# Loading the first 18 steps of a weight as 112 + 8 + 8 rows instead of 128 rows

## The chip, the cores and the metric

One core of one Trainium2 chip. The metric is device time in microseconds (us) for one execution; lower is better.

## The reference, cut to what matters

```python
q = (x @ wq)                                   # x: 8 x 576, wq: 576 x 4096
p = softmax(q . k_cache * 128**-0.5)           # 8 batches, 32 heads, 4096 keys of 128
o = p . v_cache
a = o.reshape(8, 32 * 128) @ wo                # wo: 4096 x 576  <- the weight of this case
b = gelu(layernorm(x') @ w1 + b1) @ w2 + b2    # a small MLP
out = g * a + (1 - g) * b                      # g = sigmoid(sum(x * gate_w))
```

All tensors are bf16. The two caches are 537 MB; `wo` is 4.7 MB, and it is the last thing that is loaded.

## The kernel before

The keys and values stream through three SBUF slots. `wo` goes into one of them when its last content has been used. Partition `p` of SBUF holds 32 rows of `wo`, that is 32 "steps" of 576 elements, so `wo` is 128 partition rows of 36,864 bytes. One step `j` of the last matrix product needs column group `j` of all 128 partitions. `wo` is loaded in three groups of steps (24, 6 and 2), so that the product can start on the first while the last is still on its way.

```python
    def load(engine, dst, src, name, waits=()):
        return op(engine, lambda e: e.dma_start(dst, src), waits, dma=(nc.alloc_semaphore(name), 16))
    # ... (cut)
    wo_sb = view(SL, WO_SLOT * SLOT, [128, NJO, D])      # NJO = 32 steps, D = 576
    # ... (cut)
    WO = ((0, 24), (24, 30), (30, 32))
    ld_wo = {}

    def load_wo(waits):
        w = A_wo.rearrange("(p j) n -> p j n", j=NJO)
        for n, (j0, j1) in enumerate(WO):
            t = load("sync", wo_sb[:, j0:j1, :], w[:, j0:j1, :], f"ld_wo{n}", waits)
            ld_wo.update({j: t for j in range(j0, j1)})
    # ... (cut: the loop over 32 groups; load_wo is called in its last turn)
    for j in range(NJO):
        for i in range(4):
            p_a[i] = op("tensor", lambda e, i=i, j=j: e.matmul(
                y_ps[32 * i:32 * i + B, 0:QN], lhsT=OT[:, j, :], rhs=wo_sb[:, j, i * QN:(i + 1) * QN], start=False,
                stop=(j == NJO - 1)), [ld_wo[j], *g_ot.values()])
    parts = [...]                                        # copy out of PSUM, then one store
    ld_out = [load("sync", out_flat, out_sb[:, :], "ld_out", parts)]
```

## Time and profile before

| | before |
|---|---|
| median of 3 runs | 1294.54 us (1294.54 to 1294.96) |
| span of the profiled run | 1293.1 us |
| issue of the first `wo` transfer | 1265.02 us |
| last landing of the three `wo` transfers | 1287.34, 1289.43, 1290.12 us |

The trace records each increment of a transfer's semaphore. Each of the three `wo` transfers has 16 from data, and 16 packets are in flight at a time (counted at 1278.0, 1281.0 and 1284.0 us), so one increment is read here as the landing of one DMA engine's part; "last landing" is the last of 16. The last `wo` transfer's increments run from 1288.27 to 1290.12.

The page of the kernel before, part 2, cuts the span into 40 slices. The DMA row is the busy share of the 16 DMA engines in tenths, the other row the bytes moved:

```profile
DMA  9999999999999999999999999999999999999998
GB/s 409 426 446 426 436 427 438 434 428 436 436 430 432 436 436 434 430 438 434 428 436 436 430 432 436 436 434 430 438 432 432 434 434 432 432 436 436 432 424 366
```

The DMA engines are busy from end to end. The end of the chain of waits of the kernel before (start, duration, what):

```profile
1265.02 0.33 SPq L326
...
1265.88 24.25 DMA SL<-in_A_wo_dram
1290.12 0.04 issue
1290.17 0.34 PE PS L762 x8
1290.50 0.28 DVE out_sb L765
```

The last landing of `wo` starts the last eight matmuls (L762), then a copy, then the store. Whatever moves this landing moves the time by as much. The table of windows of the kernel before, for two stretches (columns: stretch, its length, busy time of PE, PEld, DVE, ACT and POOL, clock granted to TensorE, DMA share, GB/s):

```profile
1279.00:1284.00 5.00, 4.76 (x52) 2.55 (x44) 0.00 (x0) 0.18 (x1) 0.00 (x0) 0.60 1.03 442
1288.00:1289.00 1.00, 1.00 (x68) 0.86 (x56) 0.00 (x0) 0.00 (x0) 0.00 (x0) 1.00 0.67 255
```

At the end the share falls (0.67 from 1288 to 1289, against 1.03), because the engines do not finish together: the increments of the last transfer are spread over 1.85 us. And the timeline of TensorE at the end of the kernel before (start, duration, engine, line, count, idle time before it and what ended it):

```profile
1287.38 1.68 PE L762 MATMUL PS<-SL,OT 128*8 128x144 bf16 x96 [1.85 <-DMA SL<-in_A_wo_dram]
...
1289.48 0.99 PE L762 MATMUL PS<-SL,OT 128*8 128x144 bf16 x32 [0.42 <-DMA SL<-in_A_wo_dram]
```

### The profile page before, as it was taken

The page shows a single profiled execution, that of the slowest core. Times are in us where ns is not written, and L with a number is a line of the kernel's source. Part 1 is how long each engine was busy: PE and PEld are TensorE (multiplying, and loading weights), DVE is VectorE, ACT ScalarE, POOL GpSimd, SP SyncE. Part 2 cuts the span into 40 slices and gives each one's busy share as a digit, 9 for nine tenths or more (in the row PEclk, how much of TensorE's full clock was granted, in tenths as well). Part 3 has the DMA queues.
Part 4 walks back from the last instruction along what each step waited for, and adds up shares of the span by engine and source line. Part 5 has one row for each costly group of instructions (what it writes and reads, how often), then busy time and mean ns, then how long its engine had stood idle before and what let it go on. Part 6 is the DMA issues. An engine that isn't in the chain of part 4 may idle for free.

```text
span 1293.1 us, 11630 instructions
## 1 busy us (share of the span) xinstructions
PE 721.8 (56%) x4854; PEld 330.1 (26%) x4854; DVE 814.6 (63%) x845; ACT 164.0 (13%) x597; POOL 39.7 (3%) x60
## 2 busy tenths in 40 slices
PE   3366556555556555556555556555556555556546
PEld 1122223222223222223222223222223222223223
DVE  3387567665567665567665567765567765567762
ACT  2011110011110011110011111011111011111011
POOL 1001000000000000000000000000000000000000
PEclk9588898778888877898787799778889877888888
DMA  9999999999999999999999999999999999999998
GB/s 409 426 446 426 436 427 438 434 428 436 436 430 432 436 436 434 430 438 434 428 436 436 430 432 436 436 434 430 438 432 432 434 434 432 432 436 436 432 424 366
DMA packets 10590, 557.14 MB, mean 431 GB/s; under 512 B 1201, under 2 KB 1233, under 8 KB 1745
## 3 DMA queue, kind: packets, MB, share of 16 engines
q1 hardware_dynamic: 10528, 556.94, 99.6%
q8 instruction: 8, 0.13, 0.0%
q10 hardware_dynamic: 50, 0.04, 0.0%
q14 instruction: 4, 0.03, 0.0%
HBM read 556.96 MB, written 0.01 MB: 431 GB/s over the span
## 4 chain that ended last, share of the span: by engine, by line
DMA 56%; DVE 25%; PE 13%; ACT 5%; issue 1%; SPq 0%; ACTq 0%; DVEq 0%
DMA SL<-in_A_k_cache_dram 53%; DVE SL L582 20%; PE PS L587 7%; DVE s_sb L593 5%; ACT P L625 4%; PE PS L640 4%; DMA SL<-in_A_wo_dram 2%; DMA SL<-in_A_wq_dram 1%; PE PS L656 1%; ACT O_sb L645 1%; PE PS L498 0%; PE PS L649 0%; SPq L326 0%; DVE mA L612 0%; PE PS L762 0%
## 5 line engine op out<-in xcount | busy, mean ns | idle before, releaser
L587 PE MATMUL PS<-SL,ident 128*128 128x512 bf16 x2048 | 546.8, 419 | 530.2 <-DVE SL L582 529.8
L582 DVE TENSOR_TENSOR SL<-SL,q_bc 128x4096 bf16<-128x4096 bf16 x256 | 581.8, 2283 | 328.8 <-DMA SL<-in_A_k_cache_dram 328.8
L587 PEld LDWEIGHTS PS<-SL,ident 128*128 128x128 bf16 x2048 | 198.8, 106 | 865.3 <-DVE SL L582 627.1
L593 DVE TENSOR_REDUCE s_sb<-PS 128x32 f32<-128x512 f32 x256 | 175.6, 686 | 89.8 <-PE PS L587 89.8
L625 ACT ACTIVATE P<-s_sb,hb 128x256 bf16<-128x256 f32 x256 | 126.3, 495 | 662.9 <-PE PS L640 646.4
L640 PE MATMUL PS<-SL,P 128*32 128x512 bf16 x2048 | 128.3, 388 | 0.0
L640 PEld LDWEIGHTS PS<-SL,P 128*32 128x32 bf16 x2048 | 95.6, 139 | 18.6 <-issue 2.9
L574 ACT ACTIVATE q_bc<-PS 128x128 bf16<-128x128 f32 x33 | 9.2, 277 | 420.2 <-PE PS L571 420.2
L566 POOL TENSOR_SCALAR Qm<-Q,sel 128x256 bf16<-128x256 bf16 x33 | 33.0, 1000 | 911.8 <-ACT O_sb L645 848.3
L625 ACT ACTIVATION_READ_ACCUMULATOR P<-s_sb,hb 128x1 f32 x256 | 47.9, 187 | 0.0
L656 PE MATMUL PS<-O_sb,selq 128*32 128x128 f32 x256 | 34.2, 278 | 0.7 <-ACT O_sb L645 0.7
L656 PEld LDWEIGHTS PS<-O_sb,selq 128*32 128x32 f32 x256 | 26.0, 113 | 1.4 <-ACT O_sb L645 1.2
L645 ACT ACTIVATE O_sb<-PS 128x512 f32<-128x512 f32 x32 | 18.4, 576 | 9.8 <-PE PS L640 9.8
L669 DVE SCALAR_TENSOR_TENSOR On<-PS,rz,dqm 32x128 f32<-32x128 f32 x32 | 10.9, 339 | 8.8 <-PE PS L656 7.7
L612 DVE TENSOR_REDUCE mA<-s_sb 128x1 f32<-128x256 f32 x32 | 13.4, 420 | 1.1
L683 POOL TENSOR_TENSOR OT<-OTs,g 32x96 bf16<-32x96 f32 (+2 forms) x12 | 4.2, 350 | 316.0 <-DVE OTs L673 315.9
L673 DVE TENSOR_REDUCE OTs<-On 32x32 f32<-32x128 f32 x32 | 12.0, 376 | 1.1
L522 DVE COPY SL<-PS 104x384 f32<-104x384 f32 x3 | 1.7, 553 | 16.7 <-PE PS L518 16.7
L649 PE MATMUL PS<-acc,hsel 128*32 128x8 f32 x64 | 7.4, 188 | 5.9 <-ACT O_sb L645 4.7
L663 DVE TENSOR_REDUCE zs<-PS 32x1 f32<-32x8 f32 x32 | 4.7, 148 | 8.5 <-PE PS L656 8.1
L649 PEld LDWEIGHTS PS<-acc,hsel 128*32 128x32 f32 x64 | 4.5, 110 | 19.5 <-issue 12.7
L514 PE MATMUL PS<-SL 128*8 128x384 bf16 x60 | 4.2, 430 | 7.9 <-DMA SL<-in_B_w_dram 7.9
(83 smaller groups left out, 103.4 us busy)
## 6 DMA issues: line engine op xcount, KB each, us to landing
SL<-in_A_v_cache_dram SPq DMA_DIRECT2D x2, 4096.0 KB, 38.4
SL<-in_B_w_dram SPq DMA_DIRECT2D x1, 5184.0 KB, 37.5
SL<-in_B_w_dram SPq DMA_DIRECT2D x1, 4608.0 KB, 23.9
SL<-in_A_wq_dram SPq DMA_DIRECT2D x1, 4096.0 KB, 12.8
SL<-in_A_wo_dram SPq DMA_DIRECT2D x1, 3456.0 KB, 22.3
SL<-in_A_wo_dram SPq DMA_DIRECT2D x1, 864.0 KB, 24.0
SL<-in_B_w_dram SPq DMA_DIRECT2D x1, 576.0 KB, 24.8
SL<-in_A_wq_dram SPq DMA_DIRECT2D x1, 512.0 KB, 13.4
```

Of the source, the lines that this page charges most:

```text
L566: g_qm[g] = op("gpsimd", lambda e: e.tensor_scalar(out=Qm[:, :, :].rearrange("p k d -> p (k d)"), in0=Q4[:, 2 * hg * DH:(2 * hg + 2) * DH] ...
L582: v_mult[g, c] = op("vector", lambda e: e.tensor_tensor(out=part, in0=part, in1=qb, op=ALU.mult), [land["k", g], a_qb[g]], token="tensor" ...
L587: p_sum[g, c] = op("tensor", lambda e, r=r, n=n: e.matmul(tr_ps[par][:, :], lhsT=ident[:, :], rhs=r, start=(n == 0), stop=(n == NCH - 1)), ...
L593: v_red[g, c] = op("vector", lambda e: e.tensor_reduce(out=s_sb[:, c * CT:(c + 1) * CT], in_=tr_ps[par][:, :].rearrange("p (t c) -> p t c" ...
L612: t = op("vector", lambda e: e.tensor_reduce(out=mA[:, 0:1], in_=s_sb[:, :], axis=AX.X, op=ALU.max), [v_red[g, NCK - 1], c_mA], token=own)
L625: a_exp[g] = op("scalar", lambda e, h=h: e.activation(out=P[:, :, h, :], in_=s_sb[:, :].rearrange("p (s t) -> p s t", s=2), func=ACT.Exp, ...
L640: p_pv[g] = op("tensor", lambda e, o=o, lhsT=lhsT, rhs=rhs, tq=tq: e.matmul(o, lhsT=lhsT, rhs=rhs, start=(tq < 4), stop=(tq >= NTQ - 4)), ...
L645: a_ev[g] = op("scalar", lambda e: e.activation(out=O_sb[:].rearrange("p t d -> p (t d)"), in_=o_ps[:, :], func=ACT.Copy), [p_pv[g], p_z.g ...
L649: p_z[g] = op("tensor", lambda e: e.matmul(oz_ps[0:32, DH:DH + HB], lhsT=hsel[:, :], rhs=acc[:, place(g), :], start=True, stop=True), [a_e ...
L656: p_oz[g] = op("tensor", lambda e, tt=tt: e.matmul(oz_ps[0:32, 0:DH], lhsT=selq[:, tt, :], rhs=O_sb[:, tt, :], start=(tt == 0), stop=(tt = ...
L669: t = op("vector", lambda e: e.scalar_tensor_tensor(out=On[:, :].rearrange("p (q j) -> p q j", q=NDQ), in0=oz_ps[0:32, 0:DH].rearrange("p ...
L673: v_norm[g] = op("vector", lambda e: e.tensor_reduce(out=OTs[:, :, place(g + 2)], in_=On[:, :].rearrange("p (q j) -> p j q", q=NDQ), axis= ...
```

## The change

The first 18 steps come as three transfers: rows 0 to 111, rows 112 to 119 and rows 120 to 127. The diff does not say why. The plausible intent is to even out the ragged end. Dealt out evenly, 112 rows are seven for each of 16 engines, and each transfer of 8 rows gives one more row to eight of them, so that eight carry nine rows and the others seven, in place of eight each. (The trace names no engines; the even deal is an estimate.) The groups of steps become 18, 12 and 2. The row split and the new groups are two changes in one; e1_cut_only below takes them apart.

```diff
-    WO = ((0, 24), (24, 30), (30, 32))
+    WO = ((0, 18, (0, 112, 120, 128)), (18, 30, (0, 128)), (30, 32, (0, 128)))
     ld_wo = {}
 
     def load_wo(waits):
         w = A_wo.rearrange("(p j) n -> p j n", j=NJO)
-        for n, (j0, j1) in enumerate(WO):
-            t = load("sync", wo_sb[:, j0:j1, :], w[:, j0:j1, :], f"ld_wo{n}", waits)
+        for n, (j0, j1, rows) in enumerate(WO):
+            t = [load("sync", wo_sb[p0:p1, j0:j1, :], w[p0:p1, j0:j1, :], f"ld_wo{n}_{p0}", waits)
+                 for p0, p1 in zip(rows, rows[1:])]
             ld_wo.update({j: t for j in range(j0, j1)})
...
-                stop=(j == NJO - 1)), [ld_wo[j], *g_ot.values()])
+                stop=(j == NJO - 1)), [*ld_wo[j], *g_ot.values()])
```

## The prediction

> **What bounds the kernel now.** The 16 DMA engines. The page gives queue 1 99.6% of 16 engines' span; the DMA row of the 40 slices reads 9 everywhere but the end; the chain of waits puts 56% on DMA, 25% on VectorE. wo is issued at 1265.02 us but queues behind the last V load, whose halves land at 1269.4 and 1279.1. The three wo transfers land (last of 16 semaphore increments) at 1287.34, 1289.43 and 1290.12. Then come 8 matmuls of line 762 (0.34 us), the eviction (0.28) and the output; span 1293.1. Only the landing of wo can move the time.
>
> **The tail in detail.** The 16 increments of the last transfer are spread over 1.85 us (1288.27 to 1290.12), the last 0.90 behind their mean. Engines enter wo with that spread: 1.90 us in the last V load. The window table agrees: DMA share 0.90 at 1287.4, 0.65 at 1288.2, 0.21 at 1289.0.
>
> **What the change does.** Before, each engine carries 8 of 128 rows. A row of 27,648 bytes takes 1.026 us from start to start (packet record), 27 GB/s per engine, so a row of 18 steps (20,736 bytes) is worth 0.77 us. [...] This trace agrees on the count: the 8-row loads at the start show 8 increments from data, and two of them run on the same eight packet chains. Result: engines 0-7 carry 9 rows (+0.77 us), 8-15 carry 7 (-0.77 us). Bytes are unchanged. That helps only if the late engines are in the upper half.
>
> Are they? I linked packets into 16 back-to-back chains from start to wo and marked the eight that carry the 8-row loads as engines 0-7. Near the end both halves are mixed: the latest of the lower half is 2.41 us behind one early engine, the latest of the upper half 2.69 (means 1.66 and 1.79). The lag comes mostly from single stalls of about 1 us, which hit both halves. Shifted, the lower half's latest is at 3.18 against 2.69 now: the last landing moves 0.5 us later. Near-ties leave this uncertain by about 0.1 us.
>
> **Other parts.** Two more issues (0.33 to 0.45 us each) are hidden: the queue is busy until 1277. 16 more semaphore writes of 9 ns: 0.01 us. The middle group grows from 6 to 12 steps: 56 matmuls at 15.3 ns plus 0.23 take 1.07 us from its landing, the last landing comes 0.69 us after it, so a PE backlog costs about 0.05 us. The first group's 72 matmuls are off the path. Nothing before 1265 us changes.
>
> **Predicted:** +0.55 us, 1295.1 us, range 1294.2 to 1296.1. Chances: faster by over 2% 0.005, within 2% 0.985, slower 0.01.
>
> **Right or wrong in the profile.** Five wo issues; last wo landing near 1290.6; spread of its increments up from 1.85 to about 2.5 us or more; a longer tail with DMA share near 0.5 or below; the chain still ends in wo, line 762, eviction; nothing moves in front of wo.
>
> **What would make it wrong.** If the late engines are all in the upper half, the last landing comes up to 0.7 us earlier (time near 1293.9). If the 8-row transfers take other engines, or spread over 16, nothing moves. If the stalls fall on other engines in each run, the sign varies by run.

"Engines 0-7" are the eight chains of packets that carry the 8-row loads; the trace gives no numbers. The last landing from 2.69 to 3.18 us of lag, so about +0.5, +0.05 for the backlog of TensorE and +0.01 for the semaphore writes make up the +0.55 us.

## More of the kernel before

A comparison "with before" always means the runs of the kernel before that were taken on the same chip in the same rounds.

During the first `wo` transfer the core moves 442 GB/s.

## The result, and the profile after

| | before | after |
|---|---|---|
| median of 6 runs each | 1294.75 us (1294.49 to 1295.32) | 1306.60 us (1304.90 to 1307.97) |
| ratio | | 1.009 (95% interval 1.0077 to 1.0103) |
| span of the profiled run | 1293.1 | 1304.6 |
| last landing of the first group of steps | 1287.34 | 1291.74 (112 rows), 1293.70, 1295.80 (8 rows each) |
| of the middle group | 1289.43 | 1300.21 |
| of the last group | 1290.12 | 1300.91 |
| end of the last matmul | 1290.50 | 1302.1 |

A ratio is the mean time of one kernel's runs over that of the other's runs of the same rounds, so it is not quite the ratio of the medians quoted beside it. The kernel became 11.85 us slower by the medians. That is under 1%, so it counts as "the same" at 2%, but it is far outside the predicted range and some twenty times the predicted step.

Of the 11.43 us between the two spans (1293.14 and 1304.57 in the traces), 10.79 are the later last landing and 0.64 come after it. In front of `wo` little moved: `wo` was issued at 1265.18 instead of 1265.02. One thing in front did move: the last half of the last V load landed at 1280.24 instead of 1279.11, because its slower engines were still at work when the first `wo` rows came (from 1276.60): its last packets of 32,768 bytes took up to 2.29 us, where those of before took no more than 1.22.

The page of the changed kernel, part 2:

```profile
DMA  9999999999999999999999999999999999999998
GB/s 410 441 424 439 426 437 429 438 430 438 428 434 432 436 430 436 432 436 432 434 434 434 434 434 432 436 432 436 428 440 428 436 430 434 434 434 434 432 425 213
```

The DMA row is digit for digit that of before. In the second row the first 39 numbers differ from before by at most 22 GB/s, up or down; the last has fallen from 366 to 213. The end of the chain of waits of the changed kernel:

```profile
1266.33 33.88 DMA SL<-in_A_wo_dram
1300.21 0.04 issue
1300.25 1.89 PE PS L763 x29
1302.14 0.28 DVE out_sb L766
```

The chain now leaves `wo` at the landing of the middle group, and what follows is 1.89 us of matmuls, not 0.34. The table of windows of the changed kernel, in order of time:

```profile
1279.00:1284.00 5.00, 4.52 (x53) 2.41 (x44) 0.00 (x0) 0.42 (x1) 0.00 (x0) 0.67 0.98 241
1288.00:1293.00 5.00, 0.00 (x0) 0.00 (x0) 0.00 (x0) 0.00 (x0) 0.00 (x0) 0.62 0.95 105
...
1295.50:1300.40 4.90, 2.48 (x80) 2.20 (x84) 0.00 (x0) 0.00 (x0) 0.00 (x0) 0.50 0.57 233
```

Read the last two columns together. With the 112 rows in flight the engines are 98% busy and move 241 GB/s, where before they were full as well and moved 442. With the 8-row transfers in flight they are 95% busy and move 105. The engines did not wait for work; each piece of work took longer. The packet records say the same: a packet here is one row. Before, a row of 27,648 bytes took 1.03 us and all 128 lay between 1.025 and 1.040. Now the rows of 20,736 bytes, which at that rate take 0.77 us, took 1.43 us in the median and up to 3.01; and the rows of 13,824 bytes of the middle group, which at that rate take 0.52, took up to 2.25. (Both are estimates by bytes; e1_cut_only below measured 0.77 and 0.52.) The last group's rows were unharmed: 93 ns before and after.

TensorE at the end of the changed kernel:

```profile
1296.00 2.33 PE L763 MATMUL PS<-SL,OT 128*8 128x144 bf16 x72 [10.71 <-issue]
...
1300.25 1.85 PE L763 MATMUL PS<-SL,OT 128*8 128x144 bf16 x56 [1.92 <-DMA SL<-in_A_wo_dram]
```

72 matmuls in 2.33 us, at a granted clock of 0.50; before, 96 matmuls took 1.68 us at 1.00.

### The profile page after: what moved, and what is told of

It is laid out like the page before. It is cut to its first block, busy times and chain, and to the rows that moved or that the text cites. A ratio compares the mean times of both kernels' runs of the same rounds, so it can differ in the third digit from the quotient of the medians.

```text
span 1304.6 us, 11633 instructions
## 1 busy us (share of the span) xinstructions
PE 727.1 (56%) x4854; PEld 332.9 (26%) x4854; DVE 814.6 (62%) x845; ACT 164.0 (13%) x597; POOL 39.4 (3%) x60
## 4 chain that ended last, share of the span: by engine, by line
DMA 56%; DVE 25%; PE 13%; ACT 5%; issue 1%; SPq 0%; ACTq 0%; DVEq 0%
DMA SL<-in_A_k_cache_dram 52%; DVE SL L582 20%; PE PS L587 8%; DVE s_sb L593 5%; ACT P L625 4%; PE PS L640 4%; DMA SL<-in_A_wo_dram 3%; DMA SL<-in_A_wq_dram 1%; PE PS L656 1%; ACT O_sb L645 1%; PE PS L498 0%; PE PS L649 0%; PE PS L763 0%; SPq L326 0%; DVE mA L612 0%
## 5 line engine op out<-in xcount | busy, mean ns | idle before, releaser
L763 PE MATMUL PS<-SL,OT 128*8 128x144 bf16 x128 | 4.2, 322 | 12.6 <-issue 10.7
```

## The experiments

The theory that the packets suggest (A in the expectations): what is limited is not only the DMA engine but the place in SBUF that it writes, so that rows which go to neighbouring partitions at the same time hold each other up. When the expectations were written this was the author's assumption; a packet's record has its queue, start, duration and size, but names neither its engine nor its partition. The times that remain there are estimates: 0.77 us for a row that has its place to itself, about 1.53 for two rows in one place (twice that), about 3 for four, which is also what the slowest row of the changed kernel took (3.01). The "ports" in two of the labels below come from the part that is cut; what these runs vary is the destination partitions. "Engines 0-7" is the name explained at the prediction.

The rivals: B, the new row sizes are slow to read; C, the uneven row counts or transfers on eight engines are slow in themselves; and later E, the rows are slow because of the source addresses or only because transfers overlap in the queue.

Twelve kernels ran. Each diff is against the changed kernel, except that of m_alone, which is against the kernel before. "Landing" is the last landing of the last `wo` transfer in the profiled run (1290.12 before).

| run | first 18 steps | median, us | with before, us | landing |
|---|---|---|---|---|
| e1_cut_only | 128 rows | 1294.84 | -0.1 | 1290.18 |
| e2_112_16 | 112 + 16 | 1304.37 | +9.4 | 1299.35 |
| e3_stride2 | 112 + 8 + 8, every other row | 1304.03 | +9.1 | 1298.76 |
| e4_64_64 | 64 + 64 | 1304.53 | +9.6 | 1297.93 |
| e5_96_32 | 96 + 32 | 1303.82 | +8.7 | 1297.48 |
| f1_extra_8ports | 128, and 8 + 8 extra to partitions 96,100.. and 97,101.. | 1300.02 | +4.9 | 1294.45 |
| f2_extra_2ports | 128, and 8 + 8 extra to partitions 112-119 and 120-127 | 1303.09 | +7.9 | 1297.35 |
| f4_extra_own | 128, and 8 + 8 extra to partitions 0,4.. and 1,5.. | 1297.23 | +2.2 | 1291.81 |
| e6_112_only | 112, nothing for the other 16 rows | 1300.35 | +5.4 | 1294.97 |
| after_again | the changed kernel | 1306.09 | +11.1 | 1300.36 |
| h_warm | the changed kernel, TensorE kept busy | 1304.98 | +9.8 | 1299.30 |
| m_alone | before, then eleven loads one at a time | 1372.93 (1 run) | | |

### The new groups of steps alone

```diff
-    WO = ((0, 18, (0, 112, 120, 128)), (18, 30, (0, 128)), (30, 32, (0, 128)))
+    WO = ((0, 18, (0, 128)), (18, 30, (0, 128)), (30, 32, (0, 128)))
```

> Edit: the changed step groups (18, 12, 2) with all 128 rows in one transfer each; no row split. Theory A (partition collision[...]): no collision here, so every row of 20,736 bytes takes about 0.77 us, the last wo landing is near 1290.1, time within 0.2 us of before (1294.75), at most +0.1 for the longer middle group. Rival B (the new step groups or the row sizes 20,736 and 13,824 are slow to read from HBM): packets of 20,736 bytes stay near 1.4 us and the time stays near 1300 to 1306.

Measured: 1294.84 against 1294.95 us, ratio 1.0001 (0.9985 to 1.0018). All 128 rows of 20,736 bytes took 0.771 to 0.781 us, the rows of 13,824 bytes 0.516 to 0.528. The last landing came 0.06 us later than before. So rival B is out: the row sizes cost nothing, and the whole loss is in the split of rows. The stretch in which the changed kernel moved 241 GB/s, and then TensorE in the timeline of this run:

```profile
1279.00:1284.00 5.00, 4.74 (x52) 2.51 (x44) 0.00 (x0) 0.19 (x1) 0.00 (x0) 0.60 1.01 431
...
1286.75 1.30 PE L763 MATMUL PS<-SL,OT 128*8 128x144 bf16 x72 [1.24 <-DVE OT L683]
...
1289.52 1.05 PE L763 MATMUL PS<-SL,OT 128*8 128x144 bf16 x56 [1.47 <-DMA SL<-in_A_wo_dram]
```

The 56 matmuls after the middle group take 1.05 us, as the prediction had computed (1.07).

### Even counts: 112 and 16 rows

```diff
-    WO = ((0, 18, (0, 112, 120, 128)), ...
+    WO = ((0, 18, (0, 112, 128)), ...
```

> Edit: 112 rows and one transfer of 16 rows, so every engine carries 7 + 1 = 8 rows as before; no engine is favoured. Theory A (collision): the 112 rows run as slowly as in the changed kernel (about 1.43 us a row, +4.6 us over seven rows); [...]about 3 us a row instead of 0.77 (+2.3 us). Last landing about 1297, time about 1302 (+7, with +0.8 if TensorE is cold at the end as in the changed kernel). Rival C (the loss comes from uneven row counts, engines 0-7 carrying 9 rows and 8-15 carrying 7, or from a use of only 8 engines): gone here, time within 0.5 us of before.

Measured: 1304.37, +9.4 us, where +7 was expected. m_alone's profile gives a landing (4.8 us) for its load of 16 rows, which is worked out from 16 increments, and none for its loads of 8 rows. By the reading of the increments above, 16 rows go to 16 engines; dealt out evenly, every engine carries eight rows here, as before, and no transfer runs on eight engines; rival C is out as the main cause. The median row took 1.46 us and the slowest 2.92 (the expectation's "about 3 us a row" was for the 16 rows). The size was underestimated by some 2 us.

### The same 8-row transfers, every other row

```diff
-    WO = ((0, 18, (0, 112, 120, 128)), (18, 30, (0, 128)), (30, 32, (0, 128)))
+    WO = ((0, 18, (slice(0, 112), slice(112, 128, 2), slice(113, 128, 2))), (18, 30, (slice(0, 128),)), (30, 32, (slice(0, 128),)))
# ... (cut: load_wo now takes the slices as they are)
```

> Edit: the changed kernel, but the two 8-row transfers take rows 112,114,..,126 and 113,115,..,127. Same rows in all, same engine counts, same bytes, same issues[...]. Theory A: their packets take about 1.5 us, not 2.9 to 3.0, so the two together take about 3.1 us on engines 0-7, not 6: time about 3 us below the changed kernel, near 1303.5. Rival C (uneven counts or 8 engines only): equal to the changed kernel, 1306.6 within its scatter of 3 us, and packets still near 3 us.

Measured: 1304.03 us, 2.6 below the changed kernel's 1306.60 of the earlier rounds and 2.1 below its repeat. Nine in ten rows took 1.60 us or less, against 2.01 in the changed kernel. Counts, bytes and engines are the same; only which row goes with which transfer differs. That speaks for A, though the gain is less than the 3 us expected. (The 1.5 us expected is half of the 2.9 to 3.0 of the changed kernel, for half as many rows side by side.)

### Two halves

```diff
-    WO = ((0, 18, (0, 112, 120, 128)), ...
+    WO = ((0, 18, (0, 64, 128)), ...
```

> Edit: the first 18 steps as two transfers of 64 rows, 16 engines each, 4 rows per engine. Theory A: [...]a row takes about 1.53 us while one half is in flight; 8 rows take 12.3 us instead of 6.1 if the halves run one after the other: +6.1 us, time about 1301 (up to 1302 with a cold TensorE). Some overlap between the halves at their border makes it less. Rival C: every engine has 8 rows, so equal to before. Rival B: no faster than 1.4 us a row anyway.

Measured: 1304.53 us, +9.6. The median row took 1.55 us, twice 0.77, as the expectation had it (1.53). The total was again larger than expected; the last landing alone is +7.8.

### 96 and 32 rows

```diff
-    WO = ((0, 18, (0, 112, 120, 128)), ...
+    WO = ((0, 18, (0, 96, 128)), ...
```

> Edit: the first 18 steps as 96 rows and 32 rows; 16 engines each, 6 + 2 rows per engine. Theory A: [...]about 1.53 us a row, +1.5 us over two rows. [...]+1.5 us or more if engines collide as the 112 rows did. Time about 1297.5 to 1300. Rival C (uneven counts): equal to before.

A miss in size: 1303.82 us, where 1297.5 to 1300 was expected. The median row took 1.46 us. The +1.5 us for the 96 rows rested on a count that no run shows.

### The same two extra transfers, to three places

These three kernels load all 128 rows properly and add the two 8-row transfers as extra loads into unused SBUF. Source rows, bytes, engines, order and waits are the same in all three. Only the destination partitions differ. (f4_extra_own ran later, on another chip, so it is compared by its difference from before.)

```diff
# (cut: WO as in e1_cut_only; DST stands for the two slices listed below)
+    wo_x = view(SL, WO_SLOT * SLOT + NJO * D, [128, 18, D])
# ... (cut)
+            if n == 0:
+                t += [load("sync", wo_x[d, :, :], w[s, 0:18, :], f"ld_wx{s.start}", waits)
+                      for d, s in zip(DST, (slice(112, 120), slice(120, 128)))]
# f1: DST = (slice(96, 128, 4), slice(97, 128, 4))
# f2: DST = (slice(112, 120), slice(120, 128))
# f4: DST = (slice(0, 32, 4), slice(1, 32, 4))
```

> Edit: step groups 18, 12, 2 with all 128 rows each, plus two extra 8-row loads of 18 steps (source rows 112-119 and 120-127) into unused SBUF, at partitions 96,100,..,124 and 97,101,..,125[...]. TensorE waits for them as in the changed kernel. Engines 0-7 carry two rows more than 8-15. Theory A (collision): the extra rows run at the full rate, 0.77 us each; the last landing moves about +1.25 us (2 x 0.77 on the lower half, less the 0.28 by which that half leads), time about 1296.1. Rival C (uneven counts or 8-engine transfers are slow in themselves): about as slow as its twin[...].

Measured: 1300.02 us, +4.9 where +1.25 was expected: a miss. The slowest tenth of the rows took 1.50 us and more, up to 1.58, and 49 of the 128 rows of the middle group took 0.85 to 1.1 in place of 0.52. The expectation had counted the extra rows alone, and not the rows of the 128-row transfers that were on their way at the same time. The author's guess was that some of these were being written next to the extra rows just then; the trace does not show where a packet goes.

> Edit: as its twin, same source rows, bytes, engines and order, but the extra loads go to partitions 112-119 and 120-127[...]. Theory A: their packets take about 3 us each, 6.1 us for the two in a row on engines 0-7[...]. Last landing +5 to +7 us, time about 1300.5 (1299.5 to 1303). Rival C: equal to the twin. The difference of the twins is the destination partitions alone.

Measured: 1303.09 us, +7.9, just above the expected range; the slowest rows took 2.90 us. The two kernels differ by 3.1 us for nothing but the destination partitions.

> Edit: as f1_extra_8ports, but the two extra 8-row loads go to partitions 0,4,..,28 and 1,5,..,29[...]. Same source rows, bytes, engines, order. Theory A, sharpened[...]: [...]all packets of 20,736 bytes take 0.775 us and those of 13,824 bytes 0.52; the last landing moves by about +1.3 us (two rows more on engines 0-7), time about 1296.4, 3.5 us faster than f1_extra_8ports. Rival D (8-row transfers or uneven engines cost 4 to 5 us in themselves): 1300 like f1_extra_8ports.

Measured: 1297.23 us, +2.2. All 144 rows of 20,736 bytes took 0.771 to 0.784 us: the same 8-row transfers, uneven by two rows, on eight engines, with no slow packet among them. Rival C and any cost of the source rows end here. The time is 0.8 above the expected 1296.4; the landing came +1.7 where +1.3 was expected, and TensorE was at half clock again (0.50 from 1289 to 1291; see below). One of the 128 rows of the middle group took 1.18 us; the other 127 took no more than 0.53. The same stretch in the table of windows, first of f1_extra_8ports:

```profile
1285.00:1289.00 4.00, 0.00 (x0) 0.00 (x0) 0.30 (x2) 0.00 (x0) 0.00 (x0) 0.75 0.95 221
```

then of f2_extra_2ports:

```profile
1285.00:1289.00 4.00, 0.00 (x0) 0.00 (x0) 0.63 (x3) 0.00 (x0) 0.00 (x0) 0.82 0.94 112
```

and of f4_extra_own:

```profile
1285.00:1289.00 4.00, 1.30 (x72) 1.13 (x72) 0.79 (x3) 0.00 (x0) 0.00 (x0) 0.87 0.97 400
```

About full, half and quarter rate, at a DMA share of 0.94 to 0.97 in all three. So the destination partitions alone set the rate. In f2_extra_2ports it was as low already from 1285 to 1287:

```profile
1285.00:1287.00 2.00, 0.00 (x0) 0.00 (x0) 0.63 (x3) 0.00 (x0) 0.00 (x0) 1.00 0.96 114
```

And at 1287.0 us all 16 rows in flight were slow: eight of 20,736 bytes took 2.70 to 2.82 us, eight of 13,824 bytes 1.69 to 2.09. If the extra rows had held up only each other, the eight rows of 13,824 bytes alone would have moved 213 GB/s (an estimate: eight times 13,824 bytes in the 0.52 us of e1_cut_only). The core moved half of that. So the loads into the crowded partitions held up every row in flight, also those of the next, 128-row transfer. The runs do not show how.

### Loads one at a time

```diff
+    wo_x = view(SL, WO_SLOT * SLOT + NJO * D, [128, 18, D])
+    w_src = A_wo.rearrange("(p j) n -> p j n", j=NJO)
+    t = ld_out
+    for n, parts_of in enumerate((
+            (slice(0, 128),), (slice(0, 112),), (slice(0, 96),), (slice(0, 64),), (slice(96, 128),), (slice(112, 128),),
+            (slice(112, 120), slice(120, 128)), (slice(112, 128, 2), slice(113, 128, 2)),
+            (slice(96, 128, 4), slice(97, 128, 4)), (slice(0, 32, 4), slice(1, 32, 4)), (slice(0, 128),))):
+        t = [load("sync", wo_x[r, :, :], w_src[r, 0:18, :], f"ld_t{n}_{r.start}", t) for r in parts_of]
-    op("sync", lambda e: None, ld_out)
+    op("sync", lambda e: None, t)
```

> Edit: the kernel before, with eleven timed loads of 18 steps (20,736 bytes a row) into unused SBUF after the output, each waiting for the one before, so that nothing else is in flight: rows 0-127; 0-111; 0-95; 0-63; 96-127; 112-127; 112-119 with 120-127; 112,114.. with 113,115..; 96,100.. with 97,101..; 0,4.. with 1,5..; 0-127 again. Source addresses are the same rows of wo. Theory A: a row of the 128-row load takes 0.77 us; of 0-63 and 96-127 1.5 us; of 112-127 and of 112-119/120-127 about 3 us[...]; strides 2 about 1.5; strides 4 about 0.8, in both halves now, as no other engine is at work. Loads of 112 and 96 rows between 0.8 and 1.5 us a row, near 1.4 if the changed kernel's slow rows come from these transfers alone and not from overlap with their neighbours. Rival E (slow rows come from overlap of transfers in the queue or from HBM reads of these addresses): all transfers near 0.8 us a row when alone.

From the packet records (duration from the first packet's start to the last one's end; the rate is bytes over that):

| rows | duration, us | GB/s | median row, us |
|---|---|---|---|
| 0-127 | 7.35 | 361 | 0.77 |
| 0-111 | 8.90 | 261 | 1.19 |
| 0-95 | 9.42 | 211 | 1.43 |
| 0-63 | 6.84 | 194 | 1.62 |
| 96-127 | 3.57 | 186 | 1.42 |
| 112-127 | 2.84 | 117 | 1.84 |
| 112-119, then 120-127 | 4.71 | 70 | 2.25 in the second |
| 112,114.. then 113,115.. | 3.32 | 100 | 1.55 in the second |
| 96,100.. then 97,101.. | 2.22 | 149 | 0.77 in the second |
| 0,4.. then 1,5.. | 2.40 | 138 | 0.83 in the second |
| 0-127 again | 7.42 | 358 | 0.77 |

The table of windows of this run, for the loads of 128, 112, 96 and 64 rows and of 112-119 with 120-127:

```profile
1293.40:1300.80 7.40, 0.00 (x0) 0.00 (x0) 0.00 (x0) 0.00 (x0) 0.00 (x0) 0.51 0.91 359
1302.00:1311.00 9.00, 0.00 (x0) 0.00 (x0) 0.00 (x0) 0.00 (x0) 0.00 (x0) 0.50 0.93 259
1312.40:1321.90 9.50, 0.00 (x0) 0.00 (x0) 0.00 (x0) 0.00 (x0) 0.00 (x0) 0.50 0.91 210
1323.60:1330.50 6.90, 0.00 (x0) 0.00 (x0) 0.00 (x0) 0.00 (x0) 0.00 (x0) 0.50 0.88 192
...
1342.30:1347.10 4.80, 0.00 (x0) 0.00 (x0) 0.00 (x0) 0.00 (x0) 0.00 (x0) 0.50 0.42 69
```

112 rows take longer than 128, with nothing else in flight; so do 96. Rival E is out: the short transfers are slow by themselves. The extra rows on partitions 96, 100 and so on, beside which the slowest tenth of the rows took 1.50 us and more in f1_extra_8ports, take 0.77 alone in the second of their two transfers. (In the first, which starts with nothing in flight, they took 1.21, and those on partitions 0, 4 and so on 1.19.) Two expectations missed in size: the rows of 112-119 with 120-127 and those of 112-127 were to take about 3 us and took 2.25 and 1.84. The second eight rows started over 1.3 us, one after the other, so they were not all in flight together all the time.

### How the loss divides

```diff
-    WO = ((0, 18, (0, 112, 120, 128)), ...
+    WO = ((0, 18, (0, 112)), ...
```

> Edit: the changed kernel without its two 8-row transfers; rows 112 to 127 of the first 18 steps are never loaded, so the result is wrong on purpose. Every engine has 7 rows of 18 steps, one fewer than before. Theory A: the 112 rows collide among themselves (1.19 us a row alone, 1.43 in the queue): 7 x 1.43 = 10.0 us in place of 8 x 0.775 = 6.2, so the last landing comes about +3.8 us, time about 1299.5 with a cold TensorE (1298 to 1301). The rest of the changed kernel's loss (about 11.8 - 4.6 = 7 us) is then the 8-row transfers' part. Rival: the 112 rows are slow only because the 8-row transfers behind them collide with them: then 7 rows take 5.4 us and the time is 0.8 us below before, 1294.3.

> The changed kernel itself, unedited, on the same chip and in the same rounds as e6_112_only, as a repeat of the disputed time and as its yardstick: about 1306.6 (1304.5 to 1308), with last wo landing 9 to 12 us later than before's and the 56 matmuls after the landing of the middle group in about 1.85 us.

Measured in the same rounds: 1300.35 us without the 8-row transfers, 1306.09 with them, 1294.99 for before. So the loss of 11.1 us is 5.4 from the 112-row transfer, although it carries fewer rows, and 5.7 from the two 8-row transfers. The 5.4 us contain the cold TensorE (granted clock 0.50) of the next section, since here too the 56 matmuls took 1.85 us. (The result of e6_112_only is wrong; the comparison with the reference does not see these 16 rows.) The table of windows of e6_112_only shows the reduced rate with no 8-row transfer behind it:

```profile
1279.00:1284.00 5.00, 4.29 (x55) 2.21 (x45) 0.00 (x0) 0.60 (x1) 0.00 (x0) 0.74 1.02 245
```

### TensorE at the end

```diff
     p_a = {}
+    for n in range(48):
+        op("tensor", lambda e: e.matmul(bank[6], lhsT=ident[:, :], rhs=slot[2][:, 0:4, :], start=True, stop=True),
+           list(g_ot.values()) if n == 0 else ())
     for j in range(NJO):
```

> Edit: the changed kernel with 48 dummy matmuls of 512 columns into an unused PSUM bank, after the last output norm and ahead of the wo matmuls, so that TensorE does not sit idle for 10.7 us. Theory: the TensorE clock fell to half in that idle time, so that the 56 matmuls after the landing of the middle group took 1.89 us instead of 1.07; kept busy, they take about 1.1 us again and the last matmul ends about 0.4 us after the last landing instead of 1.2. Time about 0.8 us below the changed kernel (1305.8), inside its scatter, so the trace decides. Rival: the slow matmuls come from something else (contention for SBUF); they stay at 30 ns each.

Measured: 1304.98 us. The timeline of TensorE in this run:

```profile
1286.01 10.52 PE L762 MATMUL PS<-SL,ident 128*128 128x512 bf16 x48 [1.24 <-DVE OT L683]
1296.46 1.30 PE L766 MATMUL PS<-SL,OT 128*8 128x144 bf16 x72
1298.64 1.05 PE L766 MATMUL PS<-SL,OT 128*8 128x144 bf16 x56 [0.88 <-DMA SL<-in_A_wo_dram]
```

With the 48 extra matmuls in the wait the granted clock was 1.00 from 1285 to 1299.8. The 56 matmuls take 1.05 us again, and the last one ends 0.4 us after the last landing (1299.69 against 1299.30), not 1.2. So the wait for `wo` cost a second time: idle for 10.7 us, TensorE came back at half clock. In the changed kernel the granted clock fell to 0.50 at 1289.17 us, 3.9 us after TensorE's last matmul. In f1_extra_8ports it fell 2.8 us after the last matmul. In f4_extra_own it fell from 1.00 to 0.50 at 1287.94 us, while the 72 matmuls ran (1286.69 to 1287.99), with 1.92 us of idle time before them; in e1_cut_only the same 72 matmuls ran at nearly the same time (from 1286.75, after 1.24 us) and it stayed at 1.00. How little work lets the clock fall, these runs do not show. The median is 1.6 us below the changed kernel's earlier rounds and 1.1 below its repeat. The trace accounts for 0.8; the rest lies inside that kernel's scatter of 3 us, as the landing came 1.6 us earlier in this profiled run.

No experiment points to a version that beats the kernel before, so none was run. The best splits (128 rows with other groups of steps) are equal to it.

## Why the prediction was wrong, point by point

- **Right:** the kernel is bound by DMA, and only the landing of `wo` matters. Five `wo` issues, hidden in the queue (the last at 1266.73, the first packet of `wo` at 1276.60); the chain still ends in `wo`, the matmuls, the copy. The new groups of steps cost nothing (e1_cut_only, 1.0001). Eight engines take the 8-row transfers: their semaphores show eight increments from data.
- **The step that failed:** "a row of 18 steps (20,736 bytes) is worth 0.77 us", carried over to "Result: engines 0-7 carry 9 rows (+0.77 us), 8-15 carry 7 (-0.77 us). Bytes are unchanged." The 0.77 us had been measured in transfers of 128 rows. In the changed kernel the median row took 1.43 us and the slowest 3.01. The prediction priced each engine by its own bytes and never asked where in SBUF those bytes go, nor whether one engine's rows can slow another's. The sum that it left out, by e6_112_only and after_again: 5.4 us for the 112-row transfer (the cold TensorE included) and 5.7 for the two 8-row transfers.
- **A second term mis-sized:** "a PE backlog costs about 0.05 us". True in e1_cut_only, with TensorE at full clock (1.05 us for the 56 matmuls, 1.07 computed). In the changed kernel it measured 0.8 us: 1.85 us for the 56 matmuls in place of 1.05, because the longer wait had cost TensorE its clock (0.50 granted; kept busy, in h_warm, 1.05 us at 1.00).
- **"nothing moves in front of wo"** was nearly right; the last V half landed 1.1 us later, as its last rows (up to 2.29 us in place of 1.22) met the first rows of the 112-row transfer.
- The ragged end was a true observation (1.85 us between the first and last increment), but the remedy did not work as thought. Extra rows cost little or much by where they were written: in f4_extra_own, to partitions 0, 4 and so on, all rows of that size took 0.77 to 0.78 us; in f1_extra_8ports, to 96, 100 and so on, the slowest tenth took 1.5. That a balance between engines cannot help for this reason is not shown, as no kernel tried another balance.

Left open: which rows an engine gets in a transfer of 96 or 112 rows, since the trace names neither engine nor partition of a packet, and so why these are as slow as they are; why 112 rows take 1.19 us a row alone and 1.43 in the queue; and by what path a load into crowded partitions holds up all 16 rows in flight (f2_extra_2ports at 1287.0). That the destinations are the cause is shown for the 8-row loads: with everything else equal, the rate was 400, 221 or 112 GB/s by the destination partitions alone; and alone (m_alone), the second eight rows took 2.25 us in the median to adjacent partitions, 1.55 to every other one and 0.77 or 0.83 to every fourth. What in SBUF the neighbours share is not shown. For the 112-row transfer it is shown that it is slow by itself (m_alone, e6_112_only), not why.

## What to carry to other kernels

Load SBUF with all 128 partitions in one transfer; a row range is not a smaller version of the same transfer, and here 112 rows took longer than 128 (8.90 against 7.35 us alone). A duration per row or per byte, read from one shape of transfer, holds for that shape (0.77 us a row of 128, 1.19 of 112, 1.62 of 64); before it is used for another, measure that one, as m_alone did in a single run. A small load into a few neighbouring partitions is not a small cost either: in f2_extra_2ports two of 166 KB slowed everything else in flight (rows of 0.52 us took 1.69 to 2.09). And read DMA share beside GB/s: engines that look equally busy (shares of 1.03 and 0.95) moved 442 GB/s in one kernel and 105 in the other.
